# One pool of six PSUM banks, re-estimated first transfers and new order tables in a planned attention and softplus-FFN kernel

## The chip, the cores and the metric

The kernel runs on one core of a Trainium2 chip (trn2). The metric is the device time of one execution in microseconds (us). The kernel before was timed in three runs; each kernel was also run once under the hardware profiler, and that run has a span (first to last instruction) and a time of its own.

## The reference

Inputs are f32. A causal attention with a decay per position feeds a feed-forward network (FFN) with a softplus:

```python
scores = q @ k.T / sqrt(64)                 # q, k, v: (8, 8, 576, 64)
cum = cumsum(log(clip(f, 1e-4, 1)))         # f: (8, 8, 576)
scores = where(causal, -1e9, scores + cum[:, :, :, None] - cum[:, :, None, :])
attn = softmax(scores)                      # + 1e-9 in the denominator
x = (attn @ v).transpose(0, 2, 1, 3).reshape(4608, 512)
h = x @ w_in                                # w_in: (512, 2048)
out = softplus(h) @ w_out                   # w_out: (2048, 512)
```

## The kernel before, in words

**How the work is tiled.** The 64 heads (8 batches of 8) become jobs. Batch 0 is cut by tokens, so that its first tokens go through all heads early: two "quad" jobs (four heads, 128 tokens each), four "pair" jobs (two heads, 128 further tokens) and eight jobs for the rest. The other 56 heads are one "whole" job each. Per tile of scores the chain is: scores on TensorE (L1002 in plain f32 for batch 0, with the decay sums L1020/L1021 for the quads; L1007/L1008 later), the row's minimum and the shift on VectorE (`row_min` L1012, `shift` L1049), the weight by a softplus table on ScalarE (`weight` L1056), sum and reciprocal on VectorE (L1069/L1070), a spread of the reciprocals on GpSimd (`spread`, a copy at L351), transposes back through PSUM (`b`, L1149/L1152), a copy or a split into a high and a low part (`ph`, `pl`, L351/L1171), the product with v (`o`, L1227/L1296) and a write into x (`put`, L1251).

The FFN goes by blocks of tokens: two of 128 in plain f32, one of 256, four of 512 and then two super blocks of 1024 (the instructions with `late_` in their names), whose products are formed from sums of parts. A block has the first product (`h`, `up_part`, L1516 for the plain blocks), the softplus (`gate`, L347) and the second product (`acc`, `down_part`, L1630). Most f32 operands are split into two parts, and three products are taken for one. In the first 50 us the weights arrive in pieces that ScalarE, VectorE and GpSimd turn into f32 by a chain: `load` L628 (DMA), `scale` L632 (ScalarE), `clip` L635 (VectorE), `low` L646 (GpSimd), `sign` L651 (ScalarE), `join` L657 (VectorE).

**What sets the order.** A planner (`class Plan`) holds each operation with an estimated cost on each engine that may run it, the operations it follows and the buffers it takes. It keeps a clock for each engine, takes the operation that can start soonest, and emits it; so the order of every engine's instructions, and for many operations the engine, follow from estimates. Two tables bend this: `SOONER` gives a kind of operation some us of priority, `RATHER` a kind some us for or against an engine. On the chip each engine runs its own list strictly in that order, and waits on semaphores where the estimate was too short. `PAIR` (1.4) keeps pieces of FFN work between heads from being shorter than that many us.

**PSUM.** Eight banks are three pools: `h` with two (the first product), `att` with four (scores, transposes and outputs of attention) and `acc` with two (the sums of the second product). A super block takes all of them by name. `warm` (L2661) puts twelve matmuls on the zeroed tile `halves` ahead of the first scores, in a bank of `h`; the tile is zeroed by VectorE (L495). `fill_gap` (L2673) puts matmuls of no use wherever the planner sees a gap of more than 0.15 us on TensorE, until the first operation that takes an `acc` bank:

```python
if "acc" in op.takes:
    self.fill = None
elif clock["PE"] and op.start - clock["PE"] > 0.15:
    self.fill(engines["PE"], 0.1 + 0.7 * (op.start - clock["PE"]))
```

The functions that the diff touches follow.

Of the kernel before, what the change touches and what calls it, by code (L numbers as in the profile page):

```python
# [32 lines left out]
PLAIN = 0  # L33
# [5 lines left out]
POOLB = -9.0  # L39
# [3 lines left out]
DEEP = 1  # L43
WSUMB = 0.0
DOWNB = 0.0
PAIR = 1.4
# [5 lines left out]
    "attention.finish.shift": 0.24,  # L52
    "attention.finish_stats.over early": 0.11,
    "attention.finish_stats.scale": -0.2,
    "attention.load.k": 2.33,
    "attention.load.q early": 0.41,
    "attention.load_quad.<lambda> early": 0.34,
    "attention.load_v.v": 0.78,
    "attention.load_v.v early": 0.01,
    "attention.output_tiled.put early": -0.08,  # L60
    "attention.split_v.v_hi early": -0.44,
    "attention.split_v.v_lo": 4.86,
    "attention.stat_tile.row_min": -0.1,
    "attention.stat_tile.shift": 0.18,
    "attention.stat_tile.shift early": 0.2,
    "attention.stat_tile.weight": 0.01,
    "attention.stat_tile.weight early": 0.1,
    "attention.weights.hi_part": 0.18,
    "attention.weights.lo_part": 0.16,
    "attention.weights.spread early": -0.35,  # L70
    "decay.load early": 4.01,
    "decay.log early": -4,
    "decay.store early": -0.24,
    "ffn_block.gate.hi_part": -0.21,
    "ffn_block.gate.lo_part": -0.11,
    "ffn_block.gate.raw": -0.03,
    "ffn_block.gate.raw early": -0.1,
    "ffn_block.second.load": 1.24,
    "ffn_block.split_stored.hi_part": -1.36,
    "ffn_block.split_stored.load": 1.24,  # L80
    "ffn_block.up_part.load": 0.64,
    "joined.row": 0.27,
    "load_f64.load early": 0.09,
    "load_f64.low early": -0.71,
    "load_f64.scale early": -0.02,
    "load_f64.sign early": 2.89,
    "mark": 4.55,
    "mark early": 2.26,
    "put_out.<lambda>": -0.05,
    "put_out.begin": 0.83,  # L90
    "set_rows.begin": -0.02,
    "split_w_in.hi_part": -0.12,
    "split_w_in.hi_part early": 0.11,
    "split_w_in.keep": -0.29,
    "split_w_in.keep early": -0.24,
    "split_w_in.lo_part": -0.24,
    "split_w_in.lo_part early": -0.21,
    "split_w_out.hi_part": 0.15,
    "split_w_out.hi_part early": 0.12,
    "store_x.store": -0.35,  # L100
    "super_blocks.down_set.split.low": 0.1,
    "super_blocks.down_set.sum_.<lambda>": 0.03,
    "super_blocks.gate.raw": -0.1,
    "super_blocks.lay_sums.<lambda>": 0.03,
    "super_blocks.lay_sums.low": 0.2,
    "super_blocks.lay_w.<lambda>": 5.14,
    "super_blocks.lay_w.load": 0.81,
    "super_blocks.lay_w.raw": 0.31,
    "super_blocks.lay_w.split.lo": 0.25,
    "super_blocks.lay_w.step.go": 0.16,  # L110
    "super_blocks.lay_x.less.go": 0.45,
    "super_blocks.lay_x.load": 0.05,
    "super_blocks.lay_x.split.high": -0.07,
    "super_blocks.lay_x.split.low": 3.71,
    "super_blocks.super_block.product.mm": -1.04,
    "super_blocks.super_block.ups.sum_of.go": -0.06,
    "turn_mask.turn": 0.1,
# [4 lines left out]
    ("attention.prepare.<lambda>", "DVE"): 1.23,  # L122
    ("attention.split_v.v_hi", "ACT"): -0.33,
    ("attention.weights.hi_part", "DVE"): 1.46,
    ("attention.weights.keep early", "DVE"): 2,
    ("ffn_block.gate.lo_part", "DVE"): 1.97,
    ("ffn_block.gate.lo_part", "POOL"): -0.87,
    ("load_f64.sign early", "POOL"): 0.54,
    ("put_out.<lambda>", "ACT"): -0.45,
    ("put_out.<lambda>", "DVE"): 0.08,  # L130
    ("split_w_in.hi_part early", "ACT"): -0.34,
# [223 lines left out]
def tile_decay_attention_softplus_ffn(  # L355
# [443 lines left out]
    def attention(job):  # L799
# [33 lines left out]
        def load_v(pairs=(None,)):  # L833
            for h in pairs:
# [21 lines left out]
                if h is not None:  # L856
                    more = 128, 1
# [1941 lines left out]
```

## Time and profile before

| what | value |
|---|---|
| three runs | 1119.56, 1119.87, 1120.15 us; median 1119.87 |
| profiled execution | 1120.35 us, of which the span is 1118.5 |
| TensorE (PE) busy | 1103.4 us, 99% of the span |
| VectorE (DVE), ScalarE (ACT), GpSimd (POOL) busy | 828.2, 822.2 and 526.2 us |
| largest waits of PE | 2.0 us in five times, 1.3, 1.2, 1.0, 1.0, 1.0 |

The engine rows give the time in which an engine executed something. PE is the matrix engine's stream of matmuls, and a row of it may hold several merged passes (x24 means 24 of them; a plain f32 matmul is two passes). ACTq is a sequencer: it issues DMAs. A row of waits names the instruction that waited, and what ended the wait. The granted clock (PEclk) is TensorE's clock as a share of full speed.

### The profile page before, as it was taken

Reading aid. Unit: us, or ns where it says so; the run is one execution under the profiler, and the core shown is the slowest. Engines: PE = TensorE matmul, PEld = TensorE weight load, DVE = VectorE, ACT = ScalarE, POOL = GpSimd, SP = SyncE. Lnnn points to the kernel's source line nnn. Section 1 sums busy time; section 2 is a strip of 40 time slices with the busy share of each in tenths; the row PEclk is TensorE's granted clock in tenths of the full one; section 3 lists DMA queues with packets and bytes.
Section 4 is the critical chain, followed back from the end, with each engine's and each line's share of the span. In section 5 each row is a group of like instructions: output and inputs, shape, how many; then the busy total and the mean of one; then the engine's idle time right before and its main releaser. Section 6 shows DMA issues by size and latency. Waiting matters only on the chain.

```text
span 1118.5 us, 21664 instructions
## 1 busy us (share of the span) xinstructions
PE 1103.4 (99%) x6766; PEld 955.1 (85%) x6766; DVE 828.2 (74%) x2378; ACT 822.2 (74%) x2017; POOL 526.2 (47%) x490
## 2 busy tenths in 40 slices
PE   9999999999999999999999999999999999999998
PEld 7787779888888888888888888888888788999998
DVE  4887887876676666676666866767765997998884
ACT  5898898978787898889898888787554766544431
POOL 2333687856664777746766566663010135001000
PEclk7999999999999999999999999999999999999999
DMA  7777666645446656565545755645686786443441
GB/s 195 225 224 234 213 193 203 208 153 169 147 156 193 196 166 200 165 189 168 180 151 160 233 167 172 194 140 153 213 242 199 232 222 192 149 122 122 148 123 58
DMA packets 163522, 200.54 MB, mean 179 GB/s; under 512 B 21872, under 2 KB 124560, under 8 KB 163408
## 3 DMA queue, kind: packets, MB, share of 16 engines
q1 hardware_dynamic: 163384, 199.15, 58.8%
q8 instruction: 53, 0.87, 0.3%
q14 instruction: 61, 0.50, 0.2%
q10 hardware_dynamic: 24, 0.02, 0.0%
HBM read 141.17 MB, written 57.84 MB: 178 GB/s over the span
## 4 chain that ended last, share of the span: by engine, by line
PE 85%; DVE 5%; ACT 4%; DMA 4%; issue 1%; POOL 0%; SPq 0%; ACTq 0%; DVEq 0%; POOLq 0%
PE acc L1611 17%; PE h L1537 15%; PE b L1149 8%; PE late_E L2418 7%; PE o L1296 6%; PE late_E L2081 5%; PE s L1007 3%; PE s L1008 3%; PE h L1516 2%; PE s L1002 2%; PE late_C L2081 2%; PE late_D L2081 2%; PE late_A L2081 2%; PE late_B L2418 2%; PE late_C L2418 2%; PE late_A L2418 2%
## 5 line engine op out<-in xcount | busy, mean ns | idle before, releaser
L1012 DVE CUSTOM_DVE_ANT_0 s<-s,cmask 128x288 f32<-128x288 f32 (+6 forms) x320 | 138.3, 437 | 64.4 <-PE s L1008 32.7
L1056 ACT ACTIVATE pb<-s,negm 128x288 f32<-128x288 f32 (+5 forms) x272 | 143.4, 530 | 46.6 <-DVE negm L1049 42.7
L1171 DVE TENSOR_TENSOR pl<-b,ph 128x512 fp32r<-128x512 f32 x168 | 106.8, 665 | 43.5 <-ACT ph L351 42.3
L351 ACT CAST ph<-b 64x128 fp32r<-64x128 f32 x224 | 102.5, 492 | 24.3 <-PE b L1149 22.9
L1581 POOL TENSOR_TENSOR gl<-e,gh 128x512 fp32r<-128x512 f32 x72 | 92.6, 1290 | 57.9 <-DVE gh L351 38.0
L962 POOL TENSOR_TENSOR T<-k,T 64x576 fp32r<-64x576 f32 x56 | 80.5, 1437 | 62.8 <-ACT T L351 29.2
L1007 PE MATMUL s<-T 128*128 128x192 f32 (+1 forms) x336 | 99.0, 302 | 2.2 <-ACT p L1056 2.0
L1008 PE MATMUL s<-T 68*128 68x192 f32 (+1 forms) x336 | 97.7, 295 | 0.0
L960 POOL TENSOR_TENSOR T<-q,T 64x576 fp32r<-64x576 f32 x56 | 80.3, 1434 | 25.6 <-ACT T L351 22.7
L1086 POOL TENSOR_SCALAR pb<-pb,rsum 128x320 f32<-128x320 f32 (+2 forms) x66 | 91.3, 1384 | 0.5
L1537 PE MATMUL h<-xh,wl 128*128 128x512 f32 (+1 forms) x320 | 91.2, 375 | 0.0
L1296 PE MATMUL o<-ph,vhl 128*128 128x512 f32 x336 | 88.2, 300 | 0.0
L1537 PE MATMUL h<-xh,wih 128*128 128x512 f32 (+1 forms) x320 | 81.4, 376 | 0.0
L1537 PE MATMUL h<-xl,wih 128*128 128x512 f32 (+1 forms) x320 | 79.5, 370 | 0.0
L1149 PE MATMUL b<-halves,pb 128*128 128x128 f32 x512 | 79.3, 273 | 0.0
L351 ACT CAST T<-k 128x576 fp32r<-128x576 f32 x112 | 74.9, 674 | 1.6 <-DMA k<-in_qkT 0.7
L1007 PEld LDWEIGHTS s<-T 128*128 128x128 f32 (+1 forms) x336 | 60.7, 181 | 13.3 <-ACT p L1056 4.5
L1611 PE MATMUL acc<-woh_dt_float32r,gh 128*128 128x512 f32 x176 | 71.4, 405 | 0.0
L924 POOL TENSOR_TENSOR vhl<-vr,vhl 128x384 fp32r<-128x384 f32 x56 | 57.3, 1023 | 28.2 <-ACT vhl L351 19.2
L1296 PE MATMUL o<-pl,vhl 128*128 128x512 f32 x224 | 68.9, 343 | 1.4 <-DVE pl L1171 1.3
L1611 PE MATMUL acc<-woh_dt_float32r,gl 128*128 128x512 f32 x176 | 69.2, 393 | 0.0
L1008 PEld LDWEIGHTS s<-T 68*128 68x128 f32 (+1 forms) x336 | 60.4, 180 | 10.2 <-issue 1.9
(743 smaller groups left out, 3360.2 us busy)
## 6 DMA issues: line engine op xcount, KB each, us to landing
wl<-wil_d SPq DMA_DIRECT2D x40, 512.0 KB
raw_d<-e SPq DMA_DIRECT2D x64, 256.0 KB
q<-in_qkT SPq DMA_DIRECT2D x112, 144.0 KB
k<-in_qkT SPq DMA_DIRECT2D x112, 144.0 KB
vr<-in_vR SPq DMA_DIRECT2D x64, 160.0 KB
x_d<-x SPq DMA_DIRECT2D x28, 288.0 KB
g_d<-gh SPq DMA_DIRECT2D x56, 128.0 KB
g_d<-gl SPq DMA_DIRECT2D x56, 128.0 KB
```

The source lines that it names most:

```text
L351: (e.tensor_copy if hasattr(e, "tensor_copy") else e.copy)(out, in_)
L1007: e.matmul(o, qA[:, S - end : S - q0], kA[:, a:z], start=True, stop=False)
L1008: e.matmul(o, qB[0:ST, S - end : S - q0], kB[0:ST, a:z], start=False, stop=True)
L1012: e.tensor_tensor_reduce(out=box["o"], in0=box["o"], in1=cmask[0:n_q, right - w : right], scale=-0.125, scalar=m0 if i else 3.0e38, op0=AL ...
L1056: e.activation(o, box["o"], AF.Softplus, bias=m1, scale=-1.0, accum_out=acc)
L1149: e.transpose(box["ps"][0 : x.shape[1], at : at + one.shape[1]], x, one)
L1171: e.tensor_sub(box["l"], box["ps"][:, 0:w], box["h"].bitcast(F32))
L1296: e.matmul(boxes[gi]["ps"][0:m, a:z], st["vhl"][:, c, 0:m], pbox[which][:, o : o + z - a], start=gi in fresh and which == "h", stop=gi == ...
L1537: e.matmul(o, l, r, start=m == 0, stop=m == 11)
L1611: e.matmul(st["acc", tt], l, r[fc], start=first and m == 0, stop=last and m == 2,)
L2081: e.matmul(banks[to], stationary(x, j), at(b, y, j), start=start and m == 0, stop=m == 5, skip_group_check=not start,)
L2418: e.matmul(like(o, y), x, y, start=q == 0 and f_ == 0 and m == 0, stop=q == NQ - 1 and f_ == 1 and m == 2,)
```

## The change

1. **Pools.** `BUFS` has `att=6` and no `acc`. Whatever took `acc` takes `att`: `down_part`, `second`, `finish`, and two of a super block's eight banks.
2. **Filler.** It takes its bank from `att` as an operation with no engine, gives it back at the first `up_part` (`plan.stop`), ends there and not at the first `acc`, and fills planned gaps from 0.1 us with 0.15 + 0.9 of their length.
3. **First transfers.** The planner counts the first q and k transfer of a quad as 410 KB in place of 256, and the first v of the quads as 220 in place of 128. The transfers are the same.
4. **Tables.** `PAIR` is 0, and `SOONER` and `RATHER` have new values, most of them.
5. **Code for variants.** `HYB = 8` makes `first32` (`number < nfirst + HYB`, 14) the condition where `plain` (`number < nplain`, 14) was, and `LATE_DOWN = ()` is an empty list of blocks.

```diff
-PLAIN = 0
+HYB = 8
...
+LATE_DOWN = ()
...
-PAIR = 1.4
+PAIR = 0.0
...
 SOONER = {
-    "attention.load.k": 2.33,
...
+    "attention.load.k": 5.18,
...
-                if "acc" in op.takes:
+                if op is self.stop:
                     self.fill = None
-                elif clock["PE"] and op.start - clock["PE"] > 0.15:
-                    self.fill(engines["PE"], 0.1 + 0.7 * (op.start - clock["PE"]))
+                elif clock["PE"] and op.start - clock["PE"] > 0.1:
+                    self.fill(engines["PE"], 0.15 + 0.9 * (op.start - clock["PE"]))
...
-    BUFS = dict(T=2, att=4, h=2, acc=2, fe=4, ph=3, pl=3, ph64=2, gh=LAG + 1, gl=LAG + 1, xh=1, xl=1,
+    BUFS = dict(T=2, att=6, h=2, fe=4, ph=3, pl=3, ph64=2, gh=LAG + 1, gl=LAG + 1, xh=1, xl=1,
...
-                    more = 128, 1
+                    more = 220, 1
...
-                add_dma(lambda e, h=h: qk(e, h), 256, after=[o])
+                add_dma(lambda e, h=h: qk(e, h), 410, after=[o])
...
+            if plan.stop is None:
+                plan.stop = op
+                give("att", [op])
...
-            tags = ["acc"] * len(tiles)
+            tags = ["att"] * len(tiles)
...
-                    begin(tiles, ("acc",) * 2)
+                    begin(tiles, ("att",) * 2)
...
-                put_out(f"{i}_{tt}", lambda tt=tt: st["acc", tt], rows, st["downs"][-1:], "acc")
+                put_out(f"{i}_{tt}", lambda tt=tt: st["acc", tt], rows, st["downs"][-1:], "att")
...
-                ("h", "h", "acc", "acc", "att", "att", "att", "att"),
+                ("h", "h", "att", "att", "att", "att", "att", "att"),
...
     filling = []
+    add(NO_ENGINE, lambda e: filling.append(bank("att", "fill")), takes=("att",), lag=0.0)
 
     def fill_gap(e, us):
 
-        if not filling:
-            filling.append(bank("acc", "fill"))
         for _ in range(round(us / 0.215)):
```

**What moves.** A row of order is one instruction (or several alike) of an engine's list, by its line, operation, output and inputs; in brackets are the engines or DMA lanes whose semaphores it waits for. The first place is the opening of VectorE's list. Before:

```order
L495 MEMSET halves 128x128
...
L562 MEMSET cum 64x576
L551 TENSOR_SCALAR fs<-fs 64x576 [waits DMAHW0_49]
L566 SCALAR_TENSOR_TENSOR cum<-fs 64x128 [waits Activation_49]
```

And with the change:

```order
L555 TENSOR_SCALAR fs<-fs 64x576 [waits DMAHW0_49]
L499 MEMSET halves 128x128
L570 SCALAR_TENSOR_TENSOR cum<-fs 64x128 [waits Activation_49]
```

The zeroing of `halves`, for which the warm-up waits, now stands behind the clip of f, which waits for the load of f. The other memsets go to GpSimd.

ScalarE's list at the same place holds two of the first transfers (the rows of `cum` into `T_73` for the second quad) ahead of the first softplus. Before:

```order
L887 DMA T_73<-cum 1x8x256 [waits DMAHW2_49,DVE_49]
L887 DMA T_73<-cum 1x8x256 [waits DMAHW4_49,Pool_49]
L1056 ACTIVATE pb_93,lsum_79<-s_0_0_153,negm_75 128x128 [waits DVE_49]
```

And with the change:

```order
L892 DMA T_73<-cum 1x8x256 [waits DVE_49,Pool_49]
L892 DMA T_73<-cum 1x8x256 [waits DMAHW0_49,Pool_49]
L353 COPY halves<-ident 128x64 [waits PE_49]
L353 COPY halves<-ident 128x64
L1068 ACTIVATE pb_93,lsum_79<-s_0_0_176,negm_75 128x128 [waits DVE_49]
```

The two issues no longer wait for lanes 2 and 4, which the loads of q and k use, and the copy into `halves`, which waits until the warm-up has read them, comes ahead of the softplus.

On TensorE the second quad's scores follow the first quad's sums. Before:

```order
L1002 MATMUL s_3_384_161<-T_72 128x128
L1020 MATMUL s_0_0_153<-eye8p,cum 128x128 [waits DVE_49]
L1021 MATMUL s_0_0_153<-cum,eye8m 128x128 [waits Activation_49]
...
L2673 MATMUL fill<-cmask 128x128 [waits Pool_49]
L1002 MATMUL s_0_0_204<-T_73 128x128 [waits DMAHW3_49,Activation_49]
```

And with the change:

```order
L1014 MATMUL s_3_384_182<-T_72 128x128
L1014 MATMUL s_0_0_186<-T_73 128x128 [waits DMAHW3_49]
L1032 MATMUL s_0_0_176<-eye8p,cum 128x128 [waits DVE_49]
...
L1014 MATMUL s_1_128_210<-T_73 128x128
L1014 MATMUL s_2_256_215<-T_73 128x128 [waits DMAHW4_49,Activation_49]
```

The fifth score now stands ahead of the sums and waits for its transfer alone; the sixth waits for nothing, and the seventh is the first that waits for ScalarE.

The last place is TensorE in the first product of the first super block. Before:

```order
L2081 MATMUL late_A<-late_T_10244,wih 128x512 x2
L2081 MATMUL late_A<-late_pl_10538,wih 128x512
```

And with the change:

```order
L2119 MATMUL late_A<-late_T_10184,wih 128x512 x2
L2119 MATMUL late_E_10468<-late_raw_10093,wih 128x512
L2119 MATMUL late_E_10468<-late_T_10184,wih 128x512
...
L2119 MATMUL late_D<-late_ph_10528,late_xh_10291 128x512
L2119 MATMUL late_D<-late_pl_10495,late_xh_10291 128x512
L2119 MATMUL late_A<-late_pl_10496,wih 128x512
```

22 products of other sets (`late_E`, `late_C`, `late_B`, `late_D`) now lie between the two products with `late_T` and the first that needs the split part `late_pl`.

## Rows read from the trace of the kernel before

**Rows 1.** The page: the span, the engines' busy time, and the granted clock in 40 slices of the span (tenths).

```profile
span 1118.5 us, 21664 instructions
...
PE 1103.4 (99%) x6766; PEld 955.1 (85%) x6766; DVE 828.2 (74%) x2378; ACT 822.2 (74%) x2017; POOL 526.2 (47%) x490
...
PEclk7999999999999999999999999999999999999999
```

**Rows 2.** Busy time by stretch of the span: from and to, its length, then PE, PEld, DVE, ACT and POOL busy (instructions in brackets), the granted clock of TensorE, the DMA share and GB/s.

```profile
10.00:20.00 10.00, 8.96 (x40) 7.43 (x40) 3.44 (x20) 5.50 (x23) 1.81 (x5) 0.59 0.86 286
20.00:30.00 10.00, 10.00 (x60) 7.65 (x60) 7.11 (x25) 6.88 (x16) 2.14 (x3) 0.73 0.30 100
...
40.00:200.00 160.00, 158.88 (x1078) 126.79 (x1078) 129.01 (x392) 142.52 (x350) 88.17 (x87) 1.00 0.70 216
200.00:785.00 585.00, 581.02 (x3404) 500.63 (x3403) 404.62 (x1337) 492.48 (x1294) 373.14 (x313) 1.00 0.57 174
...
820.00:960.00 140.00, 137.50 (x630) 113.59 (x629) 109.31 (x196) 84.51 (x164) 33.64 (x36) 1.00 0.75 215
```

**Rows 3.** PE's timeline up to the first FFN product: start, length, engine, line, operation, output and inputs, shapes, number of passes, and in brackets the wait before and what ended it.

```profile
1.04 4.80 PE L2661 MATMUL warm<-halves 128*128 128x128 f32 x24 [1.04 <-DVE halves L495]
...
7.48 0.38 PE L1020 MATMUL s<-eye8p,cum 64*128 64x128 f32 x2
7.71 0.38 PE L1021 MATMUL s<-cum,eye8m 64*128 64x128 f32 x2
...
11.04 0.48 PE L1002 MATMUL s<-T 64*128 64x128 f32 x2 [1.19 <-ACT pb L1056]
...
13.10 0.63 PE L1002 MATMUL s<-T 64*128 64x128 f32 x2
13.52 0.63 PE L1020 MATMUL s<-eye8p,cum 64*128 64x128 f32 x2
...
15.79 0.69 PE L1149 MATMUL b<-ident,pb 128*128 128x128 f32 x2
...
20.95 0.69 PE L1149 MATMUL b<-ident,pb 128*128 128x128 f32 x2
...
26.94 0.38 PE L1149 MATMUL b<-ident,pb 128*128 128x128 f32 x2
```

**Rows 4.** The timelines of DVE, ACT (with its DMA issues, ACTq) and POOL in the same stretch, same columns.

```profile
0.82 0.17 DVE L495 MEMSET halves<- 128x128 f32 x1 [0.82 <-PEq L2788]
...
3.53 0.45 DVE L551 TENSOR_SCALAR fs<-fs 64x576 f32<-64x576 f32 x1 [1.83 <-DMA fs<-in_f]
...
8.25 0.30 DVE L1012 CUSTOM_DVE_ANT_0 s<-s,cmask 128x128 f32<-128x128 f32 x1 [1.39 <-PE s L1021]
...
8.64 0.15 DVE L1049 TENSOR_SCALAR negm<-negm 128x1 f32<-128x1 f32 x1
...
6.97 3.50 ACTq L887 DMA_DIRECT2D T<-cum  x2
10.53 0.37 ACT L1056 ACTIVATE pb<-s,negm 128x128 f32<-128x128 f32 x1 [4.53 <-DVE negm L1049]
10.79 0.19 ACT L1056 ACTIVATION_READ_ACCUMULATOR pb<-s,negm 128x1 f32 x1
...
13.05 0.52 POOL L351 COPY one<-rsum 128x128 f32<-128x128 f32 x2 [9.39 <-DVE rsum L1070]
...
31.43 0.34 POOL L351 COPY one<-rsum 128x128 f32<-128x128 f32 x1 [6.11 <-DVE rsum L1070]
```

**Rows 5.** The timelines around the first FFN product: the last join of a piece of w_in on DVE, PE from the product to the first sum of the second product, the gate on ACT, and a join of a piece of w_out on DVE.

```profile
35.15 0.98 DVE L657 SCALAR_TENSOR_TENSOR woh_dt_float<-ti,woh_dt_float 128x512 uint32<-128x512 uint32 x1
...
36.27 3.74 PE L1516 MATMUL h<-x,woh_dt_float 128*128 128x128 f32 x32
...
41.16 0.60 PE L1149 MATMUL b<-ident,pb 128*128 128x128 f32 x4
41.60 0.27 PE L1152 MATMUL b<-ident,one 128*128 128x128 f32 x1
...
42.47 1.88 PE L1630 MATMUL acc<-wol_dt_float,g 128*128 128x512 f32 x4
...
40.04 0.60 ACT L347 ACTIVATE g<-h 128x512 f32<-128x512 f32 x1 [0.31 <-PE h L1516]
...
42.42 0.68 DVE L657 SCALAR_TENSOR_TENSOR wol_dt_float<-to,wol_dt_float 128x512 uint32<-128x512 uint32 x1
```

**Rows 6.** PE's waits over the whole span: what waited and for what, us in total, how many times, the longest.

```profile
PE s L1007 <- ACT p L1056: 2.0, 5, 0.5
PE o L1296 <- DVE pl L1171: 1.3, 1, 1.3
...
PE late_A L2081 <- ACT late_raw L351: 1.0, 1, 1.0
PE late_E L2418 <- DVE late_T L2385: 1.0, 1, 1.0
...
PE late_B L2418 <- DVE late_raw L2385: 0.3, 1, 0.3
```

**Rows 7.** PE's timeline in the first super block, around the wait of 1.0 us that Rows 6 give to `late_A`.

```profile
873.02 0.61 PE L2081 MATMUL late_A<-late_T,wih 128*128 128x512 f32 x2
874.67 0.74 PE L2081 MATMUL late_A<-late_pl,wih 128*128 128x512 f32 x2 [1.04 <-ACT late_raw L351]
```

More of the change, by code (lines that the diff above doesn't have):

```diff
@@ L77 @@
[L77 to L81, printed above, removed]
+    "attention.finish.put": 0.15,
+    "attention.finish.shift": 0.17,
+    "attention.finish_stats.over": 0.3,
+    "attention.load.k": 5.18,
+    "attention.load.k early": 4.82,
+    "attention.load.q early": 1.93,
+    "attention.load_quad.<lambda> early": 2.47,
+    "attention.load_v.v": 0.37,
@@ new lines @@
+    "attention.weights.hi_part": 0.11,
+    "attention.weights.keep early": 0.44,
+    "attention.weights.lo_part": 0.2,
+    "attention.weights.spread early": -0.65,
+    "attention.weights.turn early": 2.64,
+    "decay.clip early": 4.54,
+    "decay.load early": 0.97,
+    "decay.store early": -0.15,
+    "ffn_block.gate.hi_part": -0.3,
+    "ffn_block.gate.keep": 0.38,
+    "ffn_block.gate.raw early": 0.11,
+    "ffn_block.second.load": 5.19,
+    "ffn_block.split_stored.hi_part": 0.25,
+    "ffn_block.split_stored.load": -0.91,
@@ L107 @@
[L107 to L117, printed above, removed]
+    "super_blocks.lay_sums.low": 0.27,
+    "super_blocks.lay_w.raw": -0.72,
@@ L118 @@
+    "super_blocks.lay_w.split.hi": 0.32,
+    "super_blocks.lay_w.split.lo": 4.23,
+    "super_blocks.lay_w.step.go": 0.63,
+    "super_blocks.lay_x.less.go": 0.8,
+    "super_blocks.lay_x.load": 1.29,
+    "super_blocks.lay_x.split.high": -0.09,
+    "super_blocks.lay_x.split.low": 1.22,
+    "super_blocks.super_block.product.mm": -0.66,
+    "super_blocks.super_block.ups.moved.<lambda>": -0.49,
+    "super_blocks.super_block.ups.sum_of.go": 6,
 }
@@ L177, in __init__ @@
         self.port = "", 0.0
-        self.fill = None
+        self.fill = self.stop = None
         self.late = 0
@@ L1075, in finish_stats @@
                 st["norm"] = [st["exp"][ti] for ti in range(nt)]
-                T0_end[slot] = st["scores"]
+                if first32:
+                    T0_end.setdefault(heads[0] // 4 if quad or pair else slot // 2, []).extend(st["scores"])
                 return
@@ L1691, in second @@
                 on_pe(DM, 3 * len(tiles)), mm, after=need + st["downs"][-1:],
-                takes=("acc",) * len(tiles) if first else (),
+                takes=("att",) * len(tiles) if first else (),
             )
@@ L1715, in ffn_block @@
             ups.append(parts + [(0.0, lambda u=u: gate(u))])
-            downs.append([(down_t, lambda u=u, k=k: down_part(u, k)) for k in range(nk)])
+            downs.append([(down_t, lambda u=u, k=k: down_part(u, k)) for k in range(nk) if not raw_only])
         tail = []
-        if ahead < ntile:
+        if raw_only:
+            pass
+        elif ahead < ntile:
             downs[-2:] = [[], []]
@@ L2505, in down_out @@
                 give("fe", ends[x])
-        sets = [(s, k, q) for s in range(NSUPER) for k in range(SUPER // 256) for q in range(NQ)]
+        sets = [
+            (NSUPER + m, k, q) for m in range(len(LATE_DOWN)) for k in range(WIDE // 256) for q in range(NQ)
+        ]
+        sets += [(s, k, q) for s in range(NSUPER) for k in range(SUPER // 256) for q in range(NQ)]
         def downs(made):
@@ L2730, in tile_decay_attention_softplus_ffn @@
         if n > nstart + H:
-            later = sum(NFC * on_pe(WIDE, 24).cost for x in ready_at.values() for _ in x)
+            later = sum(
+                NFC * on_pe(WIDE, 12 if i in LATE_DOWN else 24).cost for x in ready_at.values() for i in x
+            )
             share = min(share, (here + later) / (len(jobs) - n + REST))
```

212 lines of the change are left out of this document (115 added, 97 removed).

## The prediction

> **What bounds the kernel now.** I read the page first. TensorE executes for 1103.4 of 1118.5 us, 99%, and the next engines reach 74% [rows 1]. So no gain can come from work of DVE, ACT or POOL as such: only from TensorE's own work, its clock, or the 15 us in which it stands. By the lists of order TensorE has the same matmuls after the change but for the filler. What is left to move is idle time and clock, and the second view, busy time by stretch, says where they lie [rows 2]. From 200 to 785 us TensorE lacks 4.0 us of 585, from 820 to 960 it lacks 2.5 of 140, from 40 to 200 1.1 of 160. The clock is full in these three. Between 10 and 30 us it is not: 0.59 and 0.73, that is, a part of both stretches at the 1.2 GHz level, a loss of 4.1 and 2.7 us of full clock. The opening is the worst-used part of the program, and its first FFN product starts only at 36.27 us [rows 5]. The third view, the timeline of TensorE there [rows 3], shows how the loss comes about: a wait of 1.19 us ends at 11.04, and soon behind it the same product takes twice as long (0.42 us from 13.10 to the next at 13.52, against 0.23 from 7.48 to 7.71). The fourth view, the waits, puts names on the idle time further on [rows 6].
>
> The sum is made against the profiled execution: 1118.5 of span and 1.85 around it, 1120.35, which is 0.48 above the median of the three runs. A difference of 0.2%, 2.24 us, is about what a measurement of this kernel can tell from no change.
>
> **Term A: the opening, to the first FFN product.** First what the change costs. The warm-up waits for the zeroing of `halves`, which now stands behind the clip of f. The clip ends at 3.53 + 0.45 = 3.98, the memset takes 0.17 [rows 4], so the warm-up starts at 4.2 in place of 1.04, 3.2 later, and its 4.80 us end at 9.0 [rows 3]. Five scores follow at 0.23 each, then the sums: first sums at about 10.1. Before, the first row minimum started 0.77 behind the first sums (7.48 to 8.25) and its shift ended 0.54 later [rows 3, 4]; so now the first shift is there at 11.4 and the first softplus starts at 11.4, against 10.53. Only 0.9 of the 3.2 us arrive, since before ACT was not free when the shift was: the shift ended at 8.64 + 0.15 = 8.79, but ACT was held in its two DMA issues (6.97 + 3.50 = 10.47) [rows 4], whose list shows waits for lanes that loads still used. By the new list these waits are gone.
>
> Weighed against a rule: the Trainium skill, "DMA: Bandwidth & Descriptors", section "Issuing engines are not separate DMA queues", says that starting DMAs from several engines saves the sequencer's time to issue alone, usually small beside the transfer. Here that sequencer's time was 1.74 us of ACT on the chain; if instead only the transfers counted, term A would be worse by those 1.7 us, and the sum with it.
>
> Then what it wins. Shifts follow at two products of 0.23, so the fourth softplus starts at 12.8 and its sum is read 0.45 later (10.53 to 10.79 + 0.19 [rows 4]); two small operations of DVE and a spread of half of 0.52 bring the first reciprocals to about 14.1. On TensorE five pairs of sums from 10.1 and nine products of the second quad, all at 0.23, end at 14.5, with no wait for a bank: six banks take six scores, and the seventh needs a bank that the first softplus gave back at 11.9. So the first transposes start at about 14.5, not 15.79: 1.3 earlier, and with the second quad's scores already done. That rests on the full clock, and I take it since the 1.19 us wait ahead of the fall is gone.
>
> The lead grows: behind 15.79 the next transposes came at 20.95 [rows 3], 5.2 us for what had to follow at half clock through sums, minimum, softplus and spread. Now minima and softplus of the second quad lie beside the first quad's chain, and I put them at 18.2, 2.7 earlier. Pair 1's second transposes came another 6.0 us later, at 26.94; at full clock I take 3.0 for that round too, a choice, and they come at 21.2, 5.7 earlier. The first FFN product waits for the fourth piece of w_in, whose join ends at 36.13 [rows 5]. POOL makes the last two pieces' low parts behind the spread at 31.43, which waited 6.11 us for its reciprocal [rows 4]; with the pairs 5.3 to 5.7 earlier the fourth join and the product come at about 31, 5.3 earlier. Not all of it stays. One pair's transposes that stood before the product now stand behind it: 0.60 + 0.27 = 0.9 [rows 5]. And the second product follows with no other work between, so TensorE waits for the gate, 0.60, and for the join of its piece of w_out, 0.68 [rows 5]: 1.3. Term A is -5.3 + 0.9 + 1.3 = **-3.1**. Its bounds: +3.2, if the late warm-up arrives in full, and -5.3, if nothing is given back.
>
> **Term B: the steady heads.** Of the 5.1 us that TensorE lacks between 40 and 785, two names are on record: five waits of scores for a bank that a softplus reads, 2.0, and one product `o` for its low part, 1.3 [rows 6]. With six banks in one pool a score can take a bank that the second product doesn't use, and in the new order more of TensorE's work lies between a transpose and the use of its low part. 3.3 can go. What is late next is the accumulators: they take two of the same six banks for long, and a score that met a free `att` bank before may meet none.
>
> **Term C: the super blocks.** Waits of 1.0, 1.0 and 0.3 us stand here [rows 6]. Before, the product that needs the split part followed the one before it directly, with 1.04 us of wait [rows 7]; now 22 products lie between, some 6 us of work where two take 0.61 [rows 7], and that wait is covered. 2.3 can go. What could come instead are waits at the other ends of this new order, of the same size.
>
> B and C together: 5.6 us can go, and I take half, **-2.8**, because every wait that a new order closes has before it been a planner's estimate that failed, and the new order has such estimates as well. The bounds are -5.6 and +1.5, the latter if new waits outnumber the old ones by the size of the largest, 1.3, and a little. Of the rest I cost nothing: moving casts and scales between ACT, DVE and POOL changes busy times of engines with a sixth or more of free time in the stretch from 200 to 785 (ACT 492 of 585 [rows 2]); if that cover is gone, each shows as a wait like those of rows 6. Filler passes fill gaps alone. `HYB` gives the same condition as before, `LATE_DOWN` is empty.
>
> Sum: -3.1 - 2.8 = -5.9. Span 1112.6, profiled execution 1114.45, and with the 0.48 taken off the median is **1114.0**.
>
> **Rivals.** *Rival 1, slower: the late warm-up arrives in full.* Its place is the chain from the clip of f to the first transposes; it decides when these start later than 15.79. The scores then run at half clock (0.42 for 0.23), which would happen if the warm-up, now up against waiting sums, no longer lifts the clock in time. For it: the clock at 10 to 30 us is as low as 0.59 already [rows 2]. Against it: the warm-up is as long as before and ends right at work. The price is 3.2 us: 1119.87 + 3.2 = 1123.1. The Trainium skill's page "TensorE: Matmul & The Clock Gate", section "HAM oscillation — how this bites in real kernels", says that a wait of the array brings it back to the slow clock, so the next burst starts cold; the row at 13.10, slow behind a wait, agrees, and by this rule the start at 4.2 with no idle time behind it would speak for my case and any stop before 15 us for this rival.
>
> *Rival 2, no change: the lead is handed back.* TensorE wins 5 us at the first FFN product, but the weights' conversion sets the pace behind: from 40 to 200 ACT is busy 142.5 of 160 us [rows 2]. If TensorE only waits there for pieces of weights, the end doesn't move: 1119.9. Against it: TensorE had but 1.1 us of idle time in that stretch, and an engine 89% busy has 17 us to give.
>
> *Rival 3, the shared pool.* Two of six banks go to sums, and the ten handovers of an accumulator each cost a score 0.4 us, the mean of the five bank waits (2.0 / 5 [rows 6]). That is 4.0 back: -1.9, 1118.0.
>
> That the change does nothing holds for parts alone (the variants' code; the first transfers' estimates move no transfer); the lists differ on every engine.
>
> **How the numbers follow.** My case 0.66, rival 1 0.13, rival 2 0.13, rival 3 0.08. Faster takes my case and half of rival 3, whose 1118.0 lies by the limit of 1117.6: 0.70. Same is rival 2 and the other half: 0.17. Slower is rival 1: 0.13. The range: down to 1108.5, where A reaches -5.3 and B and C -5.6 (1119.9 - 10.9 = 1109.0) with the half us by which runs differ; up to 1121.5, past rivals 2 and 3, which leaves rival 1 outside.
>
> **What would show it.** In the trace after: the warm-up at 4.2, the first softplus at 11.4, first transposes at 14.5, the first FFN product near 31 us; a granted clock above 0.59 between 10 and 20; the wait of `late_A` gone; waits of scores for softplus below 2.0 in total. A first transpose behind 15.8, or a lead at 31 us that has gone by 200, makes me wrong; so do new waits of scores for DVE's output copies, where sums give banks back.

## Result, and the profile after

The changed kernel takes 1126.12 us (median of 5 runs, 1125.47 to 1129.87), the kernel before in the same comparison 1119.56 (5 runs, 1116.74 to 1120.15). The ratio is 1.0077, 95% interval 1.0051 to 1.0103: 6.6 us slower, where 1114.0 and at most 1121.5 was forecast. The profiled execution took 1126.17 us, its span 1124.1. The runs of the kernel before differ among each other in TensorE's mean granted clock, from 0.992 to 1.000, and their times go with it (the third group of experiments).

The page after, the lines that answer to [rows 1]:

```profile
span 1124.1 us, 21657 instructions
...
PE 1101.1 (98%) x6756; PEld 949.3 (84%) x6756; DVE 842.5 (75%) x2378; ACT 821.5 (73%) x2006; POOL 516.9 (46%) x501
...
PEclk9999999999999999999999999999999999999999
```

TensorE executes 2.3 us less (among other things 36 filler passes where there were 46) in a span that is 5.6 us longer, and the page has its clock at nine tenths or more in every slice. Busy time by stretch after, columns as in [rows 2]:

```profile
10.00:20.00 10.00, 10.00 (x81) 8.95 (x81) 6.00 (x37) 6.16 (x25) 1.84 (x5) 1.00 0.90 303
20.00:30.00 10.00, 10.00 (x77) 7.49 (x76) 8.66 (x32) 8.18 (x23) 3.29 (x5) 1.00 0.53 154
30.00:40.00 10.00, 7.79 (x56) 5.75 (x54) 9.43 (x21) 7.24 (x16) 5.48 (x7) 1.00 0.85 238
40.00:200.00 160.00, 156.84 (x1064) 124.11 (x1064) 137.99 (x402) 135.90 (x336) 83.97 (x84) 1.00 0.71 216
200.00:785.00 585.00, 580.74 (x3389) 499.14 (x3388) 412.05 (x1336) 498.17 (x1301) 364.29 (x323) 1.00 0.56 172
...
820.00:960.00 140.00, 137.44 (x609) 112.43 (x608) 112.86 (x203) 80.35 (x155) 32.46 (x29) 1.00 0.71 213
```

The clock between 10 and 30 us is 1.00 where it was 0.59 and 0.73 [rows 2]. From 30 to 40 us the row of before is:

```profile
30.00:40.00 10.00, 9.29 (x80) 8.35 (x80) 9.69 (x30) 7.39 (x21) 6.01 (x8) 1.00 0.91 243
```

The new losses: TensorE lacks 2.2 us in place of 0.7 between 30 and 40, and 3.2 in place of 1.1 between 40 and 200. The opening on TensorE, to the first FFN product, columns as in [rows 3]:

```profile
4.92 5.49 PE L2711 MATMUL warm<-halves 128*128 128x128 f32 x24 [4.92 <-DVE halves L499]
...
11.78 0.38 PE L1032 MATMUL s<-eye8p,cum 64*128 64x128 f32 x2
...
16.43 0.38 PE L1165 MATMUL b<-ident,pb 128*128 128x128 f32 x2
...
20.15 0.38 PE L1165 MATMUL b<-ident,pb 128*128 128x128 f32 x2
...
23.42 0.38 PE L1165 MATMUL b<-ident,pb 128*128 128x128 f32 x2
...
30.20 0.71 PE L1533 MATMUL h<-x,woh_dt_float 128*128 128x128 f32 x4
31.47 0.49 PE L1533 MATMUL h<-x,woh_dt_float 128*128 128x128 f32 x2 [0.56 <-DVE woh_dt_float L661]
32.59 3.17 PE L1533 MATMUL h<-x,woh_dt_float 128*128 128x128 f32 x26 [0.62 <-DVE woh_dt_float L661]
36.77 1.13 PE L1666 MATMUL acc<-wol_dt_float,g 128*128 128x512 f32 x2 [1.01 <-ACT g L349]
```

The product starts at 30.20, stops twice for joins of pieces of w_in, runs from 32.59 and ends at 35.76, 4.3 earlier than before (40.01, [rows 5]); the second product waits 1.01 for the gate. The other engines' timelines (DVE, ACT, POOL) at the start, answering to [rows 4]:

```profile
3.34 1.39 DVE L555 TENSOR_SCALAR fs<-fs 64x576 f32<-64x576 f32 x1 [3.34 <-DMA fs<-in_f]
4.70 0.17 DVE L499 MEMSET halves<- 128x128 f32 x1
...
6.49 1.97 ACTq L892 DMA_DIRECT2D T<-cum  x2
...
13.12 0.37 ACT L1068 ACTIVATE pb<-s,negm 128x128 f32<-128x128 f32 x1 [2.29 <-DVE negm L1061]
...
4.18 0.24 POOL L483 MEMSET p<- 128x64 f32 x2
```

The clip takes 1.39 us where it took 0.45, and so the warm-up starts at 4.92; it runs 5.49 us, not 4.80. PE's waits from 40 us on (what waited and for what, us in total, times, longest), answering to [rows 6]:

```profile
PE b L1165 <- ACT pb L1068: 2.6, 7, 0.7
PE acc L1647 <- DMA gh_4b<-g_d: 1.3, 1, 1.3
PE late_E L2460 <- DVE late_w L2427: 1.1, 1, 1.1
PE late_E L2119 <- DMA late_wl<-wil_d: 1.0, 1, 1.0
PE s L1019 <- ACT p L1068: 0.7, 2, 0.4
PE o L1313 <- DVE pl L1188: 0.6, 2, 0.4
PE b L1165 <- POOL pb L1099: 0.6, 1, 0.6
PE late_E L2460 <- DVE late_v L2328: 0.5, 1, 0.5
```

The waits for banks fell from 2.0 us in five times to 0.7 in two, `o` for its low part from 1.3 to 0.6. In their place transposes wait for softplus weights, 2.6 us in seven times, and products for transfers that are late in the new order. Before, the same waits of transposes from 40 us on were:

```profile
PE b L1149 <- ACT pb L1056: 0.6, 2, 0.4
```

TensorE's timeline in the first super block, answering to [rows 7]:

```profile
877.98 0.61 PE L2119 MATMUL late_A<-late_T,wih 128*128 128x512 f32 x2
878.44 0.39 PE L2119 MATMUL late_E<-late_raw,wih 128*128 128x512 f32 x1
878.66 0.39 PE L2119 MATMUL late_E<-late_T,wih 128*128 128x512 f32 x1
880.09 0.50 PE L2119 MATMUL late_E<-late_raw,late_wl 128*128 128x512 f32 x1 [1.04 <-DMA late_wl<-wil_d]
```

The products of the other sets lie between, as the order shows (24 of them in the trace, not 22), and the third waits 1.04 for a load: a wait as long as before, for something else.

**Lost time.** To compare orders I added up, for each trace, the usual step of every matmul that is no warm-up and no filler (the median time from it to the next one, by line, output and shape, in the trace of before; the sum is 1077.5 us in each kernel), and took that off the time elapsed. What is left is idle time, slow clock, filler and steps longer than usual, in us, up to each time:

| kernel (see below) | 20 | 40 | 100 | 200 | 400 | 785 | 960 | 1100 |
|---|---|---|---|---|---|---|---|---|
| before | 10.7 | 18.7 | 21.7 | 26.6 | 29.8 | 32.2 | 36.1 | 36.7 |
| changed | 10.4 | 16.5 | 19.4 | 26.6 | 32.0 | 35.4 | 41.3 | 42.3 |
| order_before_pool_six | 7.9 | 11.8 | 14.3 | 18.6 | 21.7 | 24.2 | 30.0 | 30.6 |
| six_old_filler | 7.3 | 11.1 | 13.8 | 18.0 | 20.2 | 22.9 | 27.6 | 27.7 |
| two_banks_old_filler | 10.3 | 16.0 | 18.9 | 23.5 | 26.0 | 28.6 | 32.1 | 32.8 |
| changed_memsets_first | 8.4 | 15.9 | 19.2 | 26.6 | 31.7 | 37.3 | 42.6 | 43.6 |
| changed_to_200 | 8.6 | 16.4 | 19.2 | 25.3 | 30.6 | 35.5 | 39.4 | 40.0 |

The first two rows: the opening wins 2.2 us by 40, the win is gone by 200, and from there the changed order loses 5.6 more than before.

### The profile page after: what moved, and what is told of

It is laid out like the page before. It is cut to its first block, busy times and chain, and to the rows that moved or that the text cites. A ratio compares the mean times of both kernels' runs of the same rounds, so it can differ in the third digit from the quotient of the medians.

```text
span 1124.1 us, 21657 instructions
## 1 busy us (share of the span) xinstructions
PE 1101.1 (98%) x6756; PEld 949.3 (84%) x6756; DVE 842.5 (75%) x2378; ACT 821.5 (73%) x2006; POOL 516.9 (46%) x501
## 4 chain that ended last, share of the span: by engine, by line
PE 66%; DVE 4%; ACT 3%; DMA 3%; issue 1%; SPq 1%; POOL 1%; DVEq 0%; ACTq 0%; POOLq 0%
PE acc L1647 13%; PE h L1554 12%; PE late_E L2460 7%; PE late_E L2119 6%; PE o L1313 5%; PE b L1165 5%; PE s L1020 3%; PE s L1019 2%; PE late_D L2119 2%; PE late_C L2119 2%; PE late_A L2119 2%; PE late_B L2460 2%; PE late_A L2460 2%; PE late_D L2460 2%; PE late_C L2460 2%
## 5 line engine op out<-in xcount | busy, mean ns | idle before, releaser
L1024 DVE CUSTOM_DVE_ANT_0 s<-s,cmask 128x288 f32<-128x288 f32 (+6 forms) x320 | 138.8, 435 | 50.3 <-PE s L1020 22.9
L1068 ACT ACTIVATE pb<-s,negm 128x288 f32<-128x288 f32 (+5 forms) x272 | 143.8, 531 | 35.4 <-DVE negm L1061 31.5
L1601 POOL TENSOR_TENSOR gl<-e,gh 128x512 fp32r<-128x512 f32 x69 | 89.3, 1296 | 65.1 <-ACT gh L353 27.0
L353 ACT CAST ph<-b 64x128 fp32r<-64x128 f32 x224 | 100.9, 492 | 19.4 <-PE b L1165 18.3
L1363 DVE TENSOR_TENSOR x<-o,x 64x64 f32<-64x64 f32 x112 | 50.7, 454 | 46.1 <-ACT x L353 45.2
L929 POOL TENSOR_TENSOR vhl<-vr,vhl 128x384 fp32r<-128x384 f32 x56 | 56.9, 1015 | 47.0 <-ACT vhl L353 18.6
L1099 POOL TENSOR_SCALAR p<-p,rsum 64x64 f32<-64x64 f32 (+1 forms) x88 | 57.2, 661 | 39.3 <-DVE rsum L1082 16.5
L1097 ACT ACTIVATE pb<-pb,rsum 128x576 f32<-128x576 f32 (+2 forms) x105 | 69.1, 684 | 2.6 <-DVE rsum L1082 2.5
L1313 PEld LDWEIGHTS o<-ph,vhl 128*128 128x128 f32 x336 | 63.5, 189 | 7.3 <-DVE pl L1188 0.9
L1019 PEld LDWEIGHTS s<-T 128*128 128x128 f32 (+1 forms) x336 | 60.6, 180 | 10.7 <-ACT p L1068 1.5
```

The lines of the kernel that those rows point to most:

```text
L353: (e.tensor_copy if hasattr(e, "tensor_copy") else e.copy)(out, in_)
L1019: e.matmul(o, qA[:, S - end : S - q0], kA[:, a:z], start=True, stop=False)
L1024: e.tensor_tensor_reduce(out=box["o"], in0=box["o"], in1=cmask[0:n_q, right - w : right], scale=-0.125, scalar=m0 if i else 3.0e38, op0=AL ...
L1068: e.activation(o, box["o"], AF.Softplus, bias=m1, scale=-1.0, accum_out=acc)
L1313: e.matmul(boxes[gi]["ps"][0:m, a:z], st["vhl"][:, c, 0:m], pbox[which][:, o : o + z - a], start=gi in fresh and which == "h", stop=gi == ...
```

## Experiments

**Mixing the parts of the change.** The first theory was that the new tables make the new waits (theory 1), the rival that the shared pool does (theory 2), and that any new plan would lose (theory 3). In each kernel the planner plans anew.

*pool_old_tables*: the changed kernel with the old `SOONER` and `RATHER`, and

```diff
-PAIR = 0.0
+PAIR = 1.4
...
-                    more = 220, 1
+                    more = 128, 1
...
-                add_dma(lambda e, h=h: qk(e, h), 410, after=[o])
+                add_dma(lambda e, h=h: qk(e, h), 256, after=[o])
```

> The shared pool of six banks and the new filler alone: tables, PAIR 1.4 and the first transfers' estimates as before. Theory 1 (the new tables and PAIR 0 make new waits between 100 and 800 us; the opening gains 2 us): no change from before, 1118 to 1121. Theory 2 (scores wait because sums take two of six shared banks): most of the loss is here, 1123 to 1127, with waits of scores for banks. Theory 3 (any new plan loses, since the order before was the better one of many): 1122 to 1127, with waits at other places than in the changed kernel.

*early_new*: as pool_old_tables, but with the new values for the entries whose kind ends in " early" and for the estimates of the two transfers.

> The changed kernel with the tables' entries for the early phase (jobs of batch 0) and the first transfers' estimates new, the entries for the later phase and PAIR 1.4 as before. Theory 1: the opening's 2.2 us are kept, 1116 to 1119. Theory 2: 1122 to 1126. Theory 3: 1122 to 1127.

*early_old*: the other half: the early entries and the two estimates old, the later entries and `PAIR` new.

> The changed kernel with the early entries and the first transfers' estimates as before, the later entries and PAIR 0 new. Theory 1: the new waits stay and the opening's gain goes, 1127 to 1130. Theory 2: 1124 to 1127. Theory 3: anything from 1122 to 1130.

*tables_old_pools*: the kernel before with the new tables, PAIR and estimates.

> The pools of four and two banks and the old filler, with all tables, PAIR 0 and estimates new. Theory 1: nearly the changed kernel, 1124 to 1127. Theory 2: the waits go and the opening's gain stays, 1116 to 1119. Theory 3: 1122 to 1130.

Measured: 1159.51, 1170.22, 1147.71 and 1157.80 us against 1119.78 of before, ratios 1.0358, 1.0447, 1.0253 and 1.0353 (intervals within 0.004 of each). No theory had that. All four lose 28 to 50 us, four to eight times the change itself, so tables and pools can't be judged apart by planning anew. That a set of numbers fits only the one plan it was found with is the likely reading. Theory 3 came nearest, but its 1122 to 1130 was far too small.

**Following a written order.** So I wrote the order out. The planner's `run` is replaced by one that follows a list of (operation, engine), takes the first whose inputs and buffers are there, and leaves the rest as it was:

```diff
-            for op in self.ops[base : base + WINDOW]:
...
+            for at, eng in order:
+                op = self.ops[at]
+                if op.end is not None or op.missing:
+                    continue
+                if any(len(self.free[t]) < op.takes.count(t) for t in set(op.takes)):
+                    continue
+                break
```

*order_before_pool_six*: the shared pool and new filler, with the list of the kernel before.

> The shared pool of six banks, the filler stopped at the first product, and every operation in the order and on the engine that the kernel before has (the order is written out as a list and followed). Theory 4 (a bank more or less costs nothing; the loss is in the order that the tables give): the time of before, 1118 to 1121. Theory 2 (the shared pool itself makes waits): 1122 to 1126.

Measured: 1114.15 us (11 runs) against 1117.52, ratio 0.9979 (0.9961 to 0.9997). Theory 2 is wrong, and theory 4 missed something too: the shared pool with the new filler is a gain under the old order, and the table shows it in the first 40 us.

*open_new_rest_before* and *open_changed_rest_before*: the same list, with the operations of the first 90 us in pool_old_tables' order, or those of the first 60 us in the changed kernel's.

> The shared pool; the operations that the kernel before plans in its first 90 us in the order that the shared pool gives with the old tables, which opened 3 us better, and all others in the order of before. Theory 4, with a lead that lasts: 1115.5 to 1118. Theory 5 (a lead of the opening is handed back, since the weights' conversion sets the pace behind it): 1118.5 to 1121.

> The shared pool; the operations that the kernel before plans in its first 60 us in the order and on the engines of the changed kernel, late warm-up included, all others in the order of before. Theory 4 with a lead that lasts: the 2.2 us of the opening are kept, 1116.5 to 1118.5. Theory 5: 1118.5 to 1121.

Measured: 1117.65 (ratio 1.000, 0.9985 to 1.0016) and 1119.74 (1.0019, 0.9998 to 1.0039). The first lies in theory 4's range, the second in theory 5's, but neither theory knew what the pool alone gives: against the 1114.15 of the same comparison both new openings cost, 3.5 and 5.6 us. I read "no change from before" at first as a lead handed back (theory 5). The table speaks against that, since order_before_pool_six is 7.4 us ahead of before at 100 us and still 8.0 at 785. A part of the 3.5 and 5.6 is clock: both traces have it at 0.83 between 30 and 40 us, where order_before_pool_six has 1.00. The three runs of open_changed_rest_before at 1.000 took 1115.92 to 1119.23 us, the five of order_before_pool_six 1113.23 to 1114.34.

*changed_to_200*: the changed kernel's order for its first 200 us, then that of before.

> The operations that the changed kernel plans in its first 200 us in its own order, all others in the order of before; the seam itself may cost 1 to 2 us. Theory 7 (the loss has three parts, opening, 60 to 200 us and the steady heads behind 200): 4 us of waits behind 200 us go and the seam comes, 1122.5 to 1125. Rival (all of the loss is before 200 us): 1126 to 1128.

Measured: 1123.99 (11 runs; 1.0035, 1.0021 to 1.0049), inside theory 7. With the kernels above this makes steps: 1114.15, with the changed opening 1119.74, with the changed order to 200 us 1123.99, all of it 1126.12. They come from three comparisons (before 1117.52, 1119.27 and 1119.56) and hold two seams, so each step is good to some 2 us. By the ratios (0.9979, 1.0019, 1.0035, 1.0077) the steps are 4.5, 1.8 and 4.7 us, and the two intervals around the middle step overlap. All of it, from the old order to the new with the same pool and filler, is clear: 11 to 12 us. How much of it falls to each stretch is not.

**What the shared pool gains.** Over the 82 runs of the kernel before in five of the comparisons, 18 have a granted clock of 0.998 or more and a median of 1114.65 us, 64 a lower one and 1119.4. The profiled execution, at 0.994, is of the second kind. Theory 6 was the wait of the fifth score [rows 3].

*two_banks_held*: order_before_pool_six with two banks withheld from attention until the first FFN product.

```diff
+        NO_ENGINE, lambda e: filling.extend(bank("att", f"fill{i}") for i in range(2)),
+        takes=("att",) * 2, lag=0.0,
...
+            to = filling[i] if i < 2 else o
```

> As order_before_pool_six (shared pool, the order of before), with two of the six banks withheld from attention until the first FFN product: the warm-up's first two matmuls write into them and the filler uses them in turn. Attention has four banks in the opening, as before. Theory 6 (the wait of the fifth score for a bank brings TensorE to the lower clock level in most executions, and this is what the shared pool saved): the fifth score waits about 1.2 us again, runs with a granted clock of 0.993 to 0.996 come back in most rounds, and the median is 1117 to 1120. Rival (the filler's place or length did it, the banks don't count): the clock stays at 0.998 to 1.000 and the median at 1113 to 1115.

Measured: 1114.98, clock 0.999 or 1.000 in four of five runs. That looked like the rival's case, but the wait was 0.65 us, not 1.2, almost all of it because ACT came free 0.5 us sooner (the first softplus at 10.04, not 10.53); the longer filler ahead of the wait ended only 0.05 later. TensorE's row:

```profile
10.55 0.48 PE L1157 MATMUL s<-T 64*128 64x128 f32 x2 [0.65 <-ACT pb L1211]
```

The filler was next (theory 9).

*before_longer_filler* and *six_old_filler*: the kernel before with the new filler's two numbers, and order_before_pool_six with the old ones (the second edit is shown; the first is its reverse).

```diff
-                elif clock["PE"] and op.start - clock["PE"] > 0.1:
-                    self.fill(engines["PE"], 0.15 + 0.9 * (op.start - clock["PE"]))
+                elif clock["PE"] and op.start - clock["PE"] > 0.15:
+                    self.fill(engines["PE"], 0.1 + 0.7 * (op.start - clock["PE"]))
```

> The kernel before, pools of four and two banks and its own order, with the new filler's threshold (0.1) and length (0.15 + 0.9 of the gap) alone: five more filler matmuls in the opening, one of them ahead of the fifth score. Theory 9 (the filler, not the banks, holds TensorE's clock in the opening): most runs at a granted clock of 0.998 to 1.000, median 1113 to 1115.5. Rival (it takes the shared pool, too): the clock of 0.993 to 0.996 stays in most runs, median 1117 to 1120.

> order_before_pool_six with the old filler's threshold and length. Theory 9: the lower clock comes back in part of the runs, median 1115.5 to 1119. Rival (six banks take the wait away, so that no filler is needed): 1113 to 1115, clock 0.998 to 1.000.

Measured: 1119.48 (1.0009, 0.9989 to 1.0030), eight of 11 runs at 0.995 or less; and 1111.66 (0.9948, 0.9928 to 0.9968), all seven at 0.998 or more. Theory 9 is wrong both ways: the banks do it, without a longer filler, and 1111.66 is below even the rival's range. In before_longer_filler the wait is still there, and the slow steps (0.43) behind it:

```profile
11.12 0.48 PE L1002 MATMUL s<-T 64*128 64x128 f32 x2 [1.15 <-ACT pb L1056]
...
13.47 0.63 PE L1002 MATMUL s<-T 64*128 64x128 f32 x2
13.90 0.63 PE L1020 MATMUL s<-eye8p,cum 64*128 64x128 f32 x2
```

The 2.5 us between 1111.66 and 1114.15 come from two comparisons whose intervals overlap, so a cost of the longer filler is possible, not shown.

*two_banks_old_filler*: six_old_filler with the two banks withheld, which gives TensorE's list of before.

> As six_old_filler, with two of the six banks withheld until the first FFN product: the opening of TensorE's list is now that of the kernel before, one filler matmul ahead of the fifth score included. Theory 6 (the fifth score's wait for a bank, if it is long enough, brings the lower clock): a wait of 0.9 to 1.2 us, runs at 0.993 to 0.996 in most rounds, median 1115.5 to 1119. Rival (something else that the six-bank programs share): clock 0.998 to 1.000 in nearly all rounds, 1111 to 1114.

Measured: 1118.09 (11 runs; 0.9997, 0.9977 to 1.0016), all 11 runs at 0.994 to 0.997. One edit, two banks withheld until the first product (at 33 us), costs 5 to 6 us: 6.4 between the medians, which come from two comparisons, 5.5 by the ratios, whose intervals lie apart, and 5.2 between the profiled executions (1111.61 and 1116.79). TensorE's timeline of six_old_filler, and of two_banks_old_filler, at the fifth score:

```profile
9.02 0.38 PE L1176 MATMUL s<-cum,eye8m 64*128 64x128 f32 x2
9.24 0.38 PE L1157 MATMUL s<-T 64*128 64x128 f32 x2
```

```profile
9.37 0.49 PE L2871 MATMUL fill<-cmask 128*128 128x128 f32 x2
10.83 0.48 PE L1157 MATMUL s<-T 64*128 64x128 f32 x2 [0.97 <-ACT pb L1211]
...
13.30 0.63 PE L1157 MATMUL s<-T 64*128 64x128 f32 x2
13.72 0.63 PE L1175 MATMUL s<-eye8p,cum 64*128 64x128 f32 x2
```

With six banks the score follows at once. With four it waits 0.97, and some 2 us behind the wait the step from one product to the next is 0.42, the 1.2 GHz level. Busy time and clock of these kernels from 10 to 20 us say the same, first with six banks, then with four (1.00 and 0.63):

```profile
10.00:20.00 10.00, 9.87 (x76) 7.79 (x74) 7.68 (x37) 9.25 (x34) 3.85 (x8) 1.00 0.86 320
```

```profile
10.00:20.00 10.00, 9.17 (x45) 6.99 (x46) 3.98 (x23) 5.51 (x23) 1.82 (x5) 0.63 0.89 314
```

Of the six profiled executions with the order of before, the three that wait there for 0.97, 1.15 and 1.19 us have the lower clock behind it; the three that wait for 0.65 us or not at all keep the full one. Why 18 of the 82 runs of the kernel before keep it is not shown, since none of them was profiled. ACT's two issues ahead of the wait took 3.19 to 3.69 us for the same list, so a shorter wait in those runs is likely.

**What the changed opening costs.** *changed_memsets_first* puts the memsets back where they were, in the changed order; *joins_early* moves the third and fourth piece's low part, sign and join ahead in the lists of GpSimd, ScalarE and VectorE; *joins_memsets* does both. As lists of operations (0 is `halves`, 21 the clip, 104 the scale of the fifth piece):

```diff
-(20, "SP"), (21, "DVE"), ..., (0, "DVE")
+(20, "SP"), ..., (0, "DVE"), (2, "DVE"), ..., (13, "DVE"), (19, "DVE"), (21, "DVE")
```

```diff
-(104, "ACT"), ..., (70, "POOL"), (71, "ACT"), ..., (78, "POOL"), (79, "ACT"), ..., (72, "DVE"), ..., (80, "DVE")
+(70, "POOL"), (71, "ACT"), (72, "DVE"), (78, "POOL"), (79, "ACT"), (80, "DVE"), (104, "ACT")
```

> The changed kernel in its own order, but the zeroing of halves, twelve small memsets and one of cum are put on VectorE ahead of the clip of f, where they were before; the warm-up then starts at 1.0 and not 4.9, the clip takes 0.5 us and not 1.4, and the first softplus comes 3 us earlier. Theory 4 with a lead that lasts: 1122.5 to 1124.5. Theory 5: no change from the changed kernel, 1125 to 1126.5.

> The changed kernel in its order, but the low part, the sign and the join of the third and fourth piece of w_in come ahead of the attention work that stood before them on GpSimd, ScalarE and VectorE. Theory 8 (in the changed order the first FFN product is held by these joins, which end at 31.4 and 32.5 us, and that is why an earlier opening gains nothing): the product runs without a stop from 30 us, the lead grows by 2 us and stays, 1123 to 1125. Rival (the attention work put back costs as much): 1126 to 1128.

> joins_early and changed_memsets_first together. Theory 8: with the joins out of the way the early warm-up counts, the first FFN product starts near 28 us, 1121 to 1124. Rival: as the changed kernel, 1126 to 1128.

Measured: 1127.19, 1134.52 and 1131.69 (1.0091, 1.0126 and 1.0107), all above every range. In the first the clip is short again and the first FFN product comes 1.8 us earlier. DVE's row, then TensorE's (timeline):

```profile
3.43 0.45 DVE L694 TENSOR_SCALAR fs<-fs 64x576 f32<-64x576 f32 x1 [1.61 <-DMA fs<-in_f]
...
29.71 0.49 PE L1672 MATMUL h<-x,woh_dt_float 128*128 128x128 f32 x2 [0.56 <-DVE woh_dt_float L800]
30.82 4.80 PE L1672 MATMUL h<-x,woh_dt_float 128*128 128x128 f32 x26 [0.62 <-DVE woh_dt_float L800]
```

The table has it 2.0 ahead of the changed kernel at 20 us, 0.2 at 100 and level at 200: in the changed order such a lead is lost again. In this trace the first part of it goes to the clock: behind the two stops the 26 passes take 4.80 us for the 3.17 of the changed kernel, at a granted clock of 0.83 from 30 to 40 us. But the one run of five at a clock of 1.000 took 1126.41 us, no less than the changed kernel, so the clock is not all of it. Theory 8 fell: with the joins first the product ran in one piece, but from 32.70, and the gate was 2.08 late. TensorE's rows of joins_early:

```profile
32.70 3.84 PE L1672 MATMUL h<-x,woh_dt_float 128*128 128x128 f32 x32
...
38.62 1.50 PE L1805 MATMUL acc<-wol_dt_float,g 128*128 128x512 f32 x2 [2.08 <-ACT g L488]
```

What else joins_early lost is not shown.

*changed_old_filler*: the filler's two numbers set back in the changed kernel.

> The changed kernel with the old filler's threshold and length (18 filler matmuls become 13 in the opening). If the longer filler delays real work there as it did in the order of before (six_old_filler against order_before_pool_six): 1 to 2.5 us less, 1123.5 to 1125. If the changed order's opening waits for pieces of weights anyway: no change, 1125.5 to 1127.

Measured: 1126.00 (1.0070, 1.0044 to 1.0096), no change from 1126.12. The longer filler is no part of the loss that could be seen here.

## Why the prediction was wrong

**Term A** came out near its size, 18.7 - 16.5 = 2.2 us by 40 us where 3.1 was forecast, and partly by luck: a larger gain of the banks and a cost of the new order, which it didn't have, offset each other. Of its steps, the start of the warm-up was 0.7 off (4.92 for 4.2, the long clip) and its length another 0.7, the first softplus 1.7 (13.12 for 11.4) and the first transposes 1.9 (16.43 for 14.5). That is later than 15.79, so rival 1's condition was met; but the clock stayed at 1.00, and its mechanism, scores at half clock, did not come. At the full clock the opening caught up: the second quad's transposes came at 20.15, 18.2 forecast and 20.95 before, and the first product at 30.20, 31 forecast. Its two stops for joins, 1.2 us, were not in the forecast; the gate cost 1.01 (0.60 + 0.68 forecast).

The forecast had the bank wait [rows 3], its removal by six banks and the slow steps behind it. What I did not see is how large this gain is alone: two_banks_old_filler against six_old_filler gives it 5 to 6 us, and the shared pool under the old order is 18.7 - 11.8 = 6.9 us ahead by 40 us. So the changed order, which I counted as a part of the gain, costs 4.7 us in the opening (16.5 against 11.8). The comparison with one profiled execution hid that: before in its 18 runs without the lower clock is a kernel of 1114.65 us, and the change, at 0.998 or more in every run, is some 11 us behind it.

On the Trainium skill's page "TensorE: Matmul & The Clock Gate", section "HAM oscillation — how this bites in real kernels", a wait of the array for DMA, several us long, brings it back to the slow clock. The trace agrees on what follows a wait, but here a shorter one came ahead of it: two_banks_old_filler waits 0.97 us and has a clock of 0.63 from 10 to 20 us. In the changed kernel the start at 4.92 with no stop behind it stayed at 1.00, as the forecast took from that rule.

By the Trainium skill's page "DMA: Bandwidth & Descriptors", section "Issuing engines are not separate DMA queues", issue time is usually small beside the transfer: ACT is held for 1.97 us in place of 3.50, but no run here has it on the chain alone, so what it is worth stays open.

**Terms B and C** are the step that failed. I took half of 5.6 us as a gain, on the ground that an order which puts more work between two known places has fewer waits. The known ones did shrink: banks 2.0 to 0.7, the low part 1.3 to 0.6, `late_A` 1.0 to none. But the order is new at all places, not at those alone, and it made others: transposes for softplus 2.6 in place of 0.6, loads 1.3 and 1.0. From 40 us to the end the lost time is 42.3 - 16.5 = 25.8, before 36.7 - 18.7 = 18.0: +7.8 where -2.8 was forecast. The named waits account for some 4 of it (11.3 against 7.0 from 40 us on). TensorE's other idle time there is about the same (4.5 us, before 4.7), so the rest is in steps that take longer than usual while TensorE counts as busy; what holds these is not shown. Against order_before_pool_six, which differs from the changed kernel in the order and with it in the filler's places, the order costs 11.7 us: 4.7 by 40 us, 3.3 from 40 to 200 and 3.7 behind. My upper bound of +1.5 for the two terms came from the size of the largest single wait of before; it says nothing of how many new ones there are.

**Rival 2** (the lead handed back between 40 and 200) describes what happened, at the place it named, and not its reason: under the order of before the same engines keep a lead of 7.4 us. **Rival 1**'s price, 3.2 us, came nearest to the 6.6 measured, by luck, since its mechanism didn't come. **Rival 3** (the shared pool) is excluded under the order of before by order_before_pool_six; the changed order with the old pools was not tried.

Not settled: which entries of the tables make the waits behind 40 us. Mixes of the tables lose far more than the change, so no part of them was tried alone in a way that tells.

## What to carry to other kernels

Read the granted clock of all runs before taking one profile as the base: a wait of a microsecond in the opening, with the lower clock behind it, cost 5 to 6 us here, and 64 of 82 runs of the kernel before had that clock. Where a planner's numbers are tuned to one plan, test a resource with the order written out and held; planning anew lost 28 to 50 us here and answered nothing. The version that came out is the shared pool with the old order and the old filler, 1111.66 us, faster than the kernel before (0.9948, 0.9928 to 0.9968) and than the changed one (1.0077).

## What the runs showed of the hardware

VectorE's clip of 64x576 took 0.45 us or 1.39, and in both cases it ended 0.31 us after the last memset that GpSimd had under way: before at 3.98 against 3.67, changed at 4.73 against 4.42. In changed_memsets_first, with the memsets back on VectorE, it took 0.45 again and ended 0.39 after GpSimd's last. GpSimd's last memset before:

```profile
3.44 0.23 POOL L479 MEMSET p<- 128x64 f32 x2
```

Only the times are shown, not what held the clip.

The same stops need not bring the same clock. The changed kernel and changed_memsets_first both stop at the first product for 0.56 and 0.62 us; behind that the granted clock from 30 to 40 us was 1.00 in the profiled execution of the first and 0.83 in that of the second, whose row is:

```profile
30.00:40.00 10.00, 8.69 (x51) 6.83 (x51) 9.49 (x21) 6.07 (x14) 5.50 (x7) 0.83 0.75 229
```
